# A mixer kernel with linear attention on one core: spans of 384 and 288 columns, other tilings of small matmuls, and sign words from ScalarE

## The chip, the core and the metric

The kernel runs on one core of a Trainium2 chip. The metric is the device time of one execution in microseconds; the median of three runs is compared. Five engines work beside each other, each with its own queue of instructions: TensorE (PE in the profile, with its weight loads as PEld), VectorE (DVE), ScalarE (ACT), GpSimd (POOL) and SyncE (SP), which issues the transfers.

## The reference

For 4 batches, 4 heads, 1088 positions and a head size of 32, the attention is linear: queries and keys go through a product of two small projections of 8 columns each (64 features), and the sums over positions are made once per head. The result is the input of an MLP-mixer, whose weights are shared by the batches.

```python
a, b = x @ S1.T, x @ S2.T                      # 8 columns each
phi(x) = outer(a, b).reshape(64)
kv = sum_s phi(k)[f] * v[d];  z = sum_s phi(k)[f]
x = (phi(q) @ kv) / (phi(q) @ z + 1e-6)        # heads side by side: 1088 x 128
h = relu(x.T @ w_tok1) @ w_tok2                # over positions, 256 hidden
u = x + h.T
out = u + relu(u @ w_ch1) @ w_ch2              # over channels, 1536 hidden
```

All inputs are float32.

## The kernel before, in words

**Weights.** The four weight matrices and the small matrix of S1 and S2 come as 64-bit doubles, two 32-bit words per number, and are turned into float32 on the chip, in 17 pieces of 256 to 512 columns (`convert`, L279 to L319) and in one of 64 columns. ScalarE writes the magnitude of the high word (`abs`, L293) and the scaled low word (`low`, L297); VectorE clamps the magnitude (`clamp`, L300), shifts it by three bits (`shift`, L304) and puts the sign bit in (`merge`, L307); GpSimd adds the low word (`add`, L311 and L313). Then ScalarE and one of VectorE and GpSimd split the result in a high and a low float32r half (`hi`, L394, and `lo`, L397). A product with full precision is then three matmuls of halves.

**Batches.** For each batch `keys` projects the keys (`K.p`), multiplies the projections on VectorE (`K.v`) and sums over positions on TensorE (`K.s`, L460): per pair of heads and tile of 128 positions two matmuls, each with the 64 features of one head as weights and 66 columns of values of both heads. Queries of batch 0 are projected on TensorE with the small matrix spread out so that 128 feature rows come out (`Q0.p`, L539), copied by ScalarE and multiplied by VectorE or GpSimd. Queries of the other batches are projected to 8 columns (`Q.p`, L505), written to memory and read back spread out by DMA (`Q.w`, `Q.r`), then multiplied (`Q.m`). `mixing` attends (`A.x`, L645), divides (`A.d`), and does the token mixing (`A.t`, `A.w`).

**Channel mixing.** The 4352 columns of all batches are cut into spans (`_spans`): three of batch 0 (384, 384, 320), then eight of 384 and one of 192. For each span and each of 12 hidden tiles there is a group of three matmuls into a hidden bank (`U.f`, L871), a ReLU on ScalarE (`U.h`, L875), its rest on VectorE (`U.l`, L878) and three matmuls into the output bank (`U.s`, L884).

**Order.** No scheduler chooses the order: `ORDER` is a list written out by hand, with an engine behind a colon where there is a choice. `Plan.run` emits it entry by entry, and each engine takes its own entries in that order. `Plan.run` also keeps a running estimate of times, and puts matmuls on the identity (`fill`, L272) into TensorE's queue where its estimate has a hole of over 400 ns.

## Time and profile before

| | us |
|---|---|
| median of three runs (lowest, highest) | 224.02 (223.56, 224.95) |
| the profiled execution's own time | 224.45 |
| its span, first to last instruction | 222.6 |
| TensorE busy, matmuls | 216.7 |
| VectorE busy | 151.1 |
| ScalarE busy | 115.0 |
| GpSimd busy | 60.7 |

An engine is busy while one of its instructions is under way. Matmuls overlap each other, so the mean duration of one (some 0.33 us for 384 columns) is not what it costs; the spacing of starts is. A row of the timeline or of the chain that covers several instructions ends in their count. "Idle before" is idle time of the engine and what ended it.

### The profile page before, as it was taken

The numbers are of one execution on the slowest core, as the hardware profiler recorded it, in microseconds if no ns is written. First come the engines' busy times: TensorE is split into PE (matmuls) and PEld (weight loads), VectorE is DVE, ScalarE is ACT, GpSimd is POOL, SyncE is SP. The second block draws the span as 40 slices with busy tenths as digits, with TensorE's granted clock in tenths as the row PEclk, the third lists the DMA queues.
The fourth block names the chain that finished last, engine by engine and source line by source line (L and its number), as shares of the span: only waits on it lengthen the run. The fifth ranks groups of instructions, "written<-read, shape, count | busy, mean of one in ns | idle before, by whom it ended". The sixth has DMA issues, their size and how long they took to land.

```text
span 222.6 us, 4807 instructions
## 1 busy us (share of the span) xinstructions
PE 216.7 (97%) x1854; PEld 205.5 (92%) x1854; DVE 151.1 (68%) x310; ACT 115.0 (52%) x269; POOL 60.7 (27%) x62
## 2 busy tenths in 40 slices
PE   7999999999999999999999999999999999999994
PEld 7767868789899999999999999999999999999994
DVE  2599999999779854786644667384556654665652
ACT  3488859865826343444533437253554455445441
POOL 2256585578961615102120505000000000000000
PEclk9999999999999999999999999999999999999999
DMA  6999899697059884249550100035000000020001
GB/s 193 417 406 406 248 361 349 214 259 213 9 116 170 256 167 79 65 111 172 197 168 0 38 0 3 0 141 141 3 0 3 35 3 0 0 71 3 35 0 53
DMA packets 10726, 28.41 MB, mean 128 GB/s; under 512 B 1360, under 2 KB 4688, under 8 KB 10704
## 3 DMA queue, kind: packets, MB, share of 16 engines
q1 hardware_dynamic: 10704, 28.11, 41.5%
q8 instruction: 14, 0.23, 0.4%
q14 instruction: 8, 0.07, 0.1%
HBM read 23.27 MB, written 4.83 MB: 126 GB/s over the span
## 4 chain that ended last, share of the span: by engine, by line
PE 79%; DMA 6%; DVE 6%; ACT 3%; issue 2%; SPq 1%; POOL 1%; POOLq 0%; ACTq 0%
PE ps_o L884 29%; PE ps_h L871 28%; DMA br<-rows 5%; PE ps_a L821 4%; PE ps_a L701 3%; PE ps_o L272 3%; PE ps_a L645 3%; PE ps_a L460 2%; DMA doubles<-wt 2%; DVE hl L878 2%; PE ps_a L539 1%; PE ps_h L539 1%; DVE k_p L443 1%; ACT tail L297 1%; PE ps_o L460 1%
## 5 line engine op out<-in xcount | busy, mean ns | idle before, releaser
L875 ACT ACTIVATE hh<-ps_h 128x384 fp32r<-128x384 f32 (+2 forms) x144 | 68.2, 475 | 84.4 <-PE ps_h L871 63.3
L878 DVE SCALAR_TENSOR_TENSOR hl<-ps_h,hh 128x384 fp32r<-128x384 f32 (+2 forms) x144 | 75.3, 532 | 50.3 <-ACT hh L875 46.0
L871 PE MATMUL ps_h<-uh,halves 128*128 128x384 f32 (+2 forms) x288 | 86.0, 333 | 0.6 <-DVE hl L878 0.5
L884 PE MATMUL ps_o<-hh,halves 128*128 128x384 f32 (+2 forms) x288 | 72.0, 332 | 0.0
L871 PEld LDWEIGHTS ps_h<-uh,halves 128*128 128x128 f32 x288 | 53.1, 188 | 1.8 <-DVE hl L878 1.0
L884 PEld LDWEIGHTS ps_o<-hh,halves 128*128 128x128 f32 x288 | 50.6, 188 | 0.6
L871 PE MATMUL ps_h<-ul,halves 128*128 128x384 f32 (+2 forms) x144 | 47.4, 329 | 0.0
L884 PE MATMUL ps_o<-hl,halves 128*128 128x384 f32 (+2 forms) x144 | 47.4, 329 | 0.0
L871 PEld LDWEIGHTS ps_h<-ul,halves 128*128 128x128 f32 x144 | 27.1, 188 | 0.0
L884 PEld LDWEIGHTS ps_o<-hl,halves 128*128 128x128 f32 x144 | 27.1, 188 | 0.0
L625 POOL TENSOR_TENSOR qp<-qp,br 128x544 f32<-128x544 f32 x9 | 13.2, 1484 | 15.9 <-DMA br<-rows 8.7
L311 POOL TENSOR_TENSOR whole<-c,tail 128x512 int32<-128x512 int32 (+3 forms) x11 | 11.7, 1063 | 9.6 <-DVE c L307 8.1
L669 POOL TENSOR_TENSOR xl<-x,xh 128x384 fp32r<-128x384 f32 x6 | 6.1, 1017 | 28.6 <-ACT xh L665 28.6
L293 ACT ACTIVATE c<-doubles 128x512 f32<-128x512 f32 (+3 forms) x17 | 10.3, 624 | 2.5 <-DMA doubles<-wt 2.5
L443 DVE TENSOR_TENSOR k_p<-ps_a,a_sb 128x1024 f32<-128x1024 f32 (+1 forms) x12 | 11.0, 947 | 0.0
L307 DVE SCALAR_TENSOR_TENSOR c<-doubles,ps_h 128x512 int32<-128x512 int32 (+3 forms) x17 | 10.4, 610 | 0.2
L297 ACT ACTIVATE tail<-doubles 128x512 int32<-128x512 uint32 (+3 forms) x17 | 10.4, 630 | 0.1
L304 DVE TENSOR_SCALAR ps_h<-c 128x512 int32<-128x512 int32 (+3 forms) x17 | 10.3, 615 | 0.1
L645 PEld LDWEIGHTS ps_a<-kvz,qp 128*64 128x64 f32 x288 | 9.0, 137 | 1.3 <-issue 0.5
L701 PE MATMUL ps_a<-halves,xh 128*128 128x256 f32 x54 | 10.0, 279 | 0.0
L300 DVE TENSOR_SCALAR c<-c 128x512 f32<-128x512 f32 (+3 forms) x17 | 8.6, 522 | 2.0 <-ACT c L293 1.9
L313 POOL TENSOR_TENSOR c<-c,tail 128x512 int32<-128x512 int32 x6 | 8.1, 1358 | 6.6 <-DVE c L307 3.2
(82 smaller groups left out, 242.2 us busy)
## 6 DMA issues: line engine op xcount, KB each, us to landing
qp<-rows SPq DMA_DIRECT2D x6, 544.0 KB, 8.6
br<-rows SPq DMA_DIRECT2D x12, 272.0 KB
doubles<-wc SPq DMA_DIRECT2D x6, 512.0 KB, 10.8
v_sb<-v SPq DMA_DIRECT2D x4, 594.0 KB, 4.6
k_sb<-kT SPq DMA_DIRECT2D x4, 576.0 KB
q_sb<-qT SPq DMA_DIRECT2D x4, 544.0 KB, 10.4
doubles<-wt SPq DMA_DIRECT2D x4, 512.0 KB, 7.0
xm<-xb SPq DMA_DIRECT2D x3, 576.0 KB, 9.2
```

Source lines behind the costliest of these rows:

```text
L293: nc.scalar.activation(f32(t["c"]), f32(high), AF.Abs)
L297: nc.scalar.activation(t["tail"], low.bitcast(U32), AF.Copy, scale=2.0 ** -29)
L307: nc.vector.scalar_tensor_tensor(t["c"], high, -(1 << 30), t["ps"], op0=ALU.bitwise_and, op1=ALU.bitwise_or)
L311: engines[e].tensor_tensor(dst(), t["c"], t["tail"], op=ALU.add)
L443: nc.vector.tensor_tensor(t["k_p"][:pn, t0 * H:t1 * H], a.unsqueeze(3).broadcast_to([pn, n, R, R]), t["sb", t0][:pn, :n].unsqueeze(2).broa ...
L625: engines[e].tensor_tensor(qp[:, p, cs], qp[:, p, cs], t["br"][:, p, cs], op=ALU.mult)
L645: nc.tensor.matmul(x_ps[c:c + 64, o:o + 2 * (D + 1)], lhsT=qp[:, p, s0 + c:s0 + c + 64], rhs=kvz_all[b % 2][:, p, :], start=True, stop=True,)
L701: nc.tensor.matmul(t["h_ps"][:, :DTOK], lhsT=t[l][:m, i, :], rhs=part(0, piece, r, j * DTOK, DTOK)[:m], start=(i == 0 and k == 0), stop=(i ...
L871: nc.tensor.matmul(h_ps[:, :cn], lhsT=part(2, at[2][e][0], l, at[2][e][1] * P, P), rhs=r[:, :cn], start=(m == 0), stop=(m == 2))
L875: nc.scalar.activation(t["hh"][:, :cn], t["h"][:, :cn], AF.Relu)
L878: nc.vector.scalar_tensor_tensor(t["hl"][:, :cn], t["h"][:, :cn], 0.0, f32(t["hh"][:, :cn]), op0=ALU.max, op1=ALU.subtract)
L884: nc.tensor.matmul(outs[i][:, :cn], lhsT=part(3, at[3][e][0], l, at[3][e][1] * P, P), rhs=r[:, :cn], start=(e == 0 and m == 0), stop=(e == ...
```

## The change

- The last two spans have 288 and 288 columns, not 384 and 192.
- The query projection of batch 0 uses 64 rows per head pair, so that its two halves lie on different row groups of TensorE. The sums of keys and values have 33 columns, one head's values, not 66; in batches 1 to 3 they are split once more, into 32 features each on four column groups. The projection of the queries of batches 1 to 3 is cut into 64 rows by 32 columns.
- `convert` scales the magnitude by a power of two, so that its clamp needs only an upper bound; the shift moves into `merge`, and the sign words are written apart (`sign`), either by ScalarE with a parametric ReLU, or by VectorE with a mask. 13 of 18 are given to ScalarE (small matrix included).
- Identity fills cover up to 512 columns with one matmul, and 36 small matmuls (`PAD`) stand behind the first four fills. They move the later matmuls in the stream of instructions.
- Loads are no longer chained in the plan, and `ORDER` is another one. Its part up to the eighth `U.f` group is shown for both kernels.

```diff
-    for n in (384,) * 8 + (192,):
+    for n in (384,) * 7 + (288, 288):
...
-s d00 q0 k0 d01 v0 d02 d03 d04 d10 d11 d20 d30 q1 d12 d13 s.abs s.low s.clamp s.shift s.merge s.add Q0.s0:dve Q0.s1:pool w00.abs w00.low w00.clamp
-w00.shift w00.merge w00.add Q0.p00 Q0.p20 Q0.a00 Q0.a20 w01.abs Q0.p01 Q0.a01 K0.p Q0.m00 Q0.m20 w01.clamp w01.shift w01.merge Q0.p11 Q0.b01 Q0.m01
-K0.c0 K0.c4 w01.low K0.c8 w01.add w02.abs s.rows w03.abs Q0.a11 Q0.b11 w04.abs K0.v0 K0.v4 K0.v8 w02.clamp w03.clamp w02.shift w04.clamp Q0.p10 K0.s00
-K0.s04 K0.s08 K0.s10 K0.s14 K0.s18 w10.abs Q0.a10 w02.low w02.merge w10.clamp w03.shift Q0.m10 w03.merge Q0.m11 Q0.p21 K0.kvz w03.low w02.add w04.low
-A0.x0 w03.add Q0.a21 Q0.b21 w10.low w11.abs w20.abs Q0.m21 A0.x1 w04.shift w10.shift A0.d0 A0.d1 w04.merge w11.clamp w04.add w10.merge w11.shift
-w20.clamp w11.merge Q1.p Q1.c0 w11.low w30.low w10.add w11.add w13.low w12.abs Q1.c1 w30.abs w20.low w12.low w13.abs A0.x2 A0.d2 A0.t0 A0.t1 A0.t2
-A0.relu A0.hT A0.hTh A0.u0 A0.w0 k1 d21 d31 Q1.w0 v1 Q1.w1 d14 d15 d22 d32 q2 w20.shift w12.clamp w30.clamp w20.merge w13.clamp w12.shift w30.shift
-w12.merge w13.shift w30.merge w20.add w20.hi A0.uh00 K1.p w12.add w20.lo:dve w30.add A0.ul00 w13.merge U0.f U0.f A0.u1 U0.f w13.add A0.w1 w00.hi K1.c0
-K1.c8 w30.hi U0.h U0.h w21.abs U0.h w21.low A0.uh11 w30.lo:pool K1.v0 K1.v8 U0.l U0.l w21.clamp U0.l w21.shift A0.ul11 w21.merge U0.s U0.s U0.s U1.f
-U1.f U1.f w04.hi K1.c4 w14.abs w22.abs w31.low U1.h w31.abs w21.add K1.v4 Q2.p K1.s U1.h w21.hi Q2.c0 U1.h w14.low Q2.c1 w15.low k2 K2.p U1.l
-w14.clamp w31.clamp w31.shift w22.clamp U1.l w31.merge U1.l w14.shift w14.merge w22.shift w22.merge Q1.r0None Q1.r00 Q1.r01 v2 Q1.r1None Q1.r10 Q1.r11
-Q2.w0 q3 k3 w21.lo:pool U0.f U0.f U1.s U1.s U1.s U0.f w31.add w32.abs w32.low K1.kvz w31.hi U0.h w14.add w15.abs U0.h U0.l w32.clamp U0.l w32.shift
...
+s q0 d00 d01 k0 s.low s.abs s.clamp s.sign:act s.merge s.add Q0.s0:dve Q0.s1:dve s.rows Q0.p00 Q0.p01 Q0.a00 Q0.m00 Q0.a01 Q0.b01 Q0.m01 w00.sign:dve
+Q0.p20 Q0.p21 w00.abs Q0.a20 Q0.m20 w00.clamp w01.abs Q0.a21 Q0.b21 v0 d04 d02 d03 w01.clamp w00.merge w01.sign:dve w01.merge Q0.p10 Q0.a10 K0.p
+Q0.p11 w01.low w00.low Q0.m21 w00.add w01.add K0.c0 K0.c4 w04.low w04.abs Q0.a11 K0.c8 Q0.b11 w02.abs w02.sign:act w03.abs w02.low K0.v0 K0.v4 K0.v8
+w02.clamp Q0.m10 d11 d20 d10 d12 q1 d13 d30 k1 Q0.m11 w02.merge w03.sign:act w03.clamp w04.clamp w03.merge K0.s00 K0.s04 K0.s08 K0.s10 K0.s14 K0.s18
+K0.kvz A0.x0 w04.sign:act w03.low w11.abs w11.sign:act w11.low w04.merge w02.add w04.add A0.d0 A0.x1 w11.clamp A0.d1 w11.merge A0.x2 A0.t0 A0.t1 A0.d2
+Q1.p w03.add w20.sign:act w11.add w10.abs w12.abs w20.low w20.abs w10.sign:act w10.low w13.abs w13.sign:act Q1.c0 Q1.c1 w13.low w12.low w10.clamp
+w20.clamp w12.clamp w10.merge w13.clamp w20.merge A0.t2 A0.relu A0.hT w12.sign:dve w12.merge w13.merge w10.add w20.add w30.sign:act w30.abs A0.hTh
+w30.clamp w30.merge w12.add K1.p d21 v1 d15 d31 d32 Q1.w0 Q1.w1 d14 d22 q2 Q1.r0None Q1.r00 Q1.r01 Q1.r1None Q1.r10 Q1.r11 w13.add w20.hi K1.c0
+w30.low w21.abs K1.c8 K1.c4 K1.v0 w21.clamp w20.lo:pool A0.u0 A0.w0 A0.u1 A0.w1 w21.sign:act A0.uh00 K1.v8 w21.merge A0.ul00 K1.v4 U0.f U0.f w04.hi
+w21.low w31.sign:act w31.abs A0.uh11 w30.add w21.add U0.h U0.h w30.hi K1.s A0.ul11 U0.l w31.clamp U0.l w31.merge w30.lo:pool w31.low w21.hi w31.add
+U0.f U1.f A0.u2 U0.h U1.h w15.abs w14.abs U0.l U1.l U1.f U0.s U1.f U0.s U0.s U1.s U1.h K1.kvz w31.hi w15.clamp w14.sign:dve w14.clamp U1.l
+w15.sign:act U1.h w21.lo:pool w14.merge w15.merge U1.l w32.abs w32.sign:act U0.f U0.f U1.s w32.clamp w32.merge w31.lo:pool U0.h U0.l w22.sign:dve Q2.p
...
+PAD = 36
...
-LEAST = 2.0 ** -15
-MOST = 122879.9921875
+REBIAS = 2.0 ** -112
+MOST = 2.0 ** -95 * (1 - 2.0 ** -24)
...
-            for _ in range(n):
-                nc.tensor.matmul(spare_ps[:, :P], lhsT=ident, rhs=ident, start=True, stop=True)
+            for w in [4] * (n // 4) + [1] * (n % 4):
+                nc.tensor.matmul(spare_ps[:, :w * P], lhsT=ident, rhs=ident.unsqueeze(1).broadcast_to([P, w, P]), start=True, stop=True)
...
-            nc.scalar.activation(f32(t["c"]), f32(high), AF.Abs)
+            nc.scalar.activation(f32(t["c"]), f32(high), AF.Abs, scale=REBIAS)
...
+        def sign(e):
+            t["ps"] = bank("ps_h")[:, :n].bitcast(I32)
+            if e == "act":
+                nc.scalar.activation(t["ps"], f32(high), AF.Prelu, scale=2.0 ** -19, alpha=2.0 ** 70)
+            else:
+                nc.vector.tensor_scalar(t["ps"], high, -(1 << 31), None, op0=ALU.bitwise_and)
+
         def clamp(_):
-            nc.vector.tensor_scalar(f32(t["c"]), f32(t["c"]), LEAST, MOST, op0=ALU.max, op1=ALU.min)
-
-        def shift(_):
-            t["ps"] = bank("ps_h").bitcast(I32)[:, :n]
-            nc.vector.tensor_scalar(t["ps"], t["c"], 3, 0x3FFFFFFF, op0=ALU.logical_shift_left, op1=ALU.bitwise_and)
+            nc.vector.tensor_scalar_min(f32(t["c"]), f32(t["c"]), MOST)
 
         def merge(_):
-            nc.vector.scalar_tensor_tensor(t["c"], high, -(1 << 30), t["ps"], op0=ALU.bitwise_and, op1=ALU.bitwise_or)
+            nc.vector.scalar_tensor_tensor(t["c"], t["c"], 3, t["ps"], op0=ALU.logical_shift_left, op1=ALU.bitwise_or)
...
+                    parts = 2 if b else 1
                     for j in range(2):
                         h = 2 * p + j
-                        nc.tensor.matmul(
-                            t["kv"][j * F:(j + 1) * F, p * 2 * (D + 1):(p + 1) * 2 * (D + 1)],
-                            lhsT=t["k_p"][:n, i * H + h].rearrange("p i j -> p (i j)"),
-                            rhs=t["v"][:n, i, 2 * p:2 * p + 2, :].rearrange("p h d -> p (h d)"),
-                            start=(i == 0), stop=(i == NT - 1),
-                        )
+                        for c in range(parts):
+                            o, m = j * F + c * F // parts, F // parts
+                            nc.tensor.matmul(
+                                t["kv"][o:o + m, p * (D + 1):(p + 1) * (D + 1)],
+                                lhsT=t["k_p"][:n, i * H + h, c * R // parts:(c + 1) * R // parts].rearrange("p i j -> p (i j)"),
+                                rhs=t["v"][:n, i, h, :], start=(i == 0), stop=(i == NT - 1),
+                            )
...
-    def project_queries(q, r, ps):
-        for j in range(2):
-            c = 2 * j + r
-            nc.tensor.matmul(ps[j * 64:(j + 1) * 64, :QC], lhsT=box["s_rows"], rhs=q[:, c * QC:(c + 1) * QC], start=True, stop=True)
+    def project_queries(q, ps):
+        for c in range(4):
+            for p in range(2):
+                rows = slice(p * 64, (p + 1) * 64)
+                nc.tensor.matmul(ps[p][c * 32:(c + 1) * 32, :QC], lhsT=box["s_rows"][rows], rhs=q[rows, c * QC:(c + 1) * QC], start=True, stop=True)
...
+                    for p in range(2):
+                        rows = slice(p * 64, (p + 1) * 64)
+                        nc.tensor.matmul(
+                            t[kind, g, p][:, :cn], lhsT=t["s"][rows, kind, 2 * p:2 * p + 2].rearrange("p h i j -> p (h i j)"),
+                            rhs=box["q_sb", 0][rows, cs], start=True, stop=True,
+                        )
...
+    for i in range(PAD):
+        c = i % 4 * 32
+        nc.tensor.matmul(spare_ps[c:c + 32, :8], lhsT=ident[:, c:c + 32], rhs=ident[:, :8], start=True, stop=True)
```

## Rows read from the trace of the kernel before

**Rows 1.** The page: busy time per engine, the queue of TensorE's instructions

```profile
PE 216.7 (97%) x1854; PEld 205.5 (92%) x1854; DVE 151.1 (68%) x310; ACT 115.0 (52%) x269; POOL 60.7 (27%) x62
...
q8 instruction: 14, 0.23, 0.4%
```

**Rows 2.** Busy time (count) by stretch: PE, PEld, DVE, ACT, POOL; clock; DMA

```profile
5.54:44.04 38.50, 37.28 (x452) 29.55 (x450) 35.50 (x71) 30.26 (x72) 20.83 (x18) 1.00 0.93 342
44.04:219.60 175.56, 175.21 (x1386) 171.79 (x1386) 114.15 (x235) 83.05 (x195) 38.24 (x34) 1.00 0.31 80
```

**Rows 3.** The chain of waits around 47 us: start, length, what

```profile
44.62 0.69 DVE c L307
...
47.07 0.79 PE ps_h L871 x3
```

**Rows 4.** TensorE's timeline, first 30 us: start, length, instruction, count

```profile
1.36 6.70 PE L272 MATMUL ps_o<-ident 128*128 128x128 f32 x32 [1.36 <-POOL ident masks.py:199]
7.90 0.81 PE L539 MATMUL ps_a<-q_sb,s_spread 128*128 128x384 f32 x2
...
15.63 2.32 PE L460 MATMUL ps_o<-v_sb,k_p 128*64 128x66 f32 x72
...
20.71 0.94 PE L272 MATMUL ps_o<-ident 128*128 128x128 f32 x6
...
27.68 0.38 PE L272 MATMUL ps_o<-ident 128*128 128x128 f32 x2
```

**Rows 5.** TensorE's timeline, a wait, and the second matmul of the eighth group

```profile
43.11 0.45 PE L871 MATMUL ps_h<-uh,halves 128*128 128x384 f32 x1 [0.35 <-DVE hl L878]
...
44.31 0.34 PE L871 MATMUL ps_h<-ul,halves 128*128 128x384 f32 x1
```

**Rows 6.** The chain of waits, matmuls of 320, 384 and 192 columns

```profile
80.38 0.88 PE ps_h L871 x6
...
191.21 1.56 PE ps_h L871 x9
...
214.18 0.67 PE ps_h L871 x6
```

**Rows 7.** Busy time of L539, the query projection of batch 0

```profile
7.00:24.00 17.00, 8.01 (x24) 4.32 (x24) 1.00 1.03 408
```

**Rows 8.** TensorE's timeline: a look ending at 56.68; sums of batch 2 and their surroundings

```profile
56.67 0.28 PE L460 MATMUL ps_a<-v_sb,k_p 128*64 128x66 f32 x2
...
81.19 1.14 PE L505 MATMUL ps_a<-q_sb,s_rows 128*64 128x272 f32 x8
82.15 2.27 PE L460 MATMUL ps_a<-v_sb,k_p 128*64 128x66 f32 x72
84.35 0.56 PE L884 MATMUL ps_o<-hh,halves 128*128 128x320 f32 x2
84.75 0.31 PE L884 MATMUL ps_o<-hl,halves 128*128 128x320 f32 x1
```

**Rows 9.** Groups by form: low word and table load (ScalarE), shift (VectorE); busy us, mean ns

```profile
L297 ACT ACTIVATE tail<-doubles 128x512 int32<-128x512 uint32 x10 | 6.9, 686 | 0.0
...
L297 ACT ACTIVATE tail<-doubles 128x384 int32<-128x384 uint32 x4 | 2.3, 572 | 0.1
...
L293 ACT ACT_TABLE_LOAD x1 | 1.3, 1283 | 0.7 <-PEq L983 0.7
...
L304 DVE TENSOR_SCALAR ps_h<-c 128x512 int32<-128x512 int32 x10 | 6.9, 686 | 0.1
...
L304 DVE TENSOR_SCALAR ps_h<-c 128x384 int32<-128x384 int32 x4 | 2.2, 552 | 0.0
```

**Rows 10.** ScalarE's timeline: two conversions that follow each other

```profile
5.54 0.67 ACT L293 ACTIVATE c<-doubles 128x512 f32<-128x512 f32 x1 [2.54 <-DMA doubles<-wt]
6.11 0.67 ACT L297 ACTIVATE tail<-doubles 128x512 int32<-128x512 uint32 x1
```

**Rows 11.** The end: the last add, which waits for the last matmul

```profile
219.57 0.35 DVE L909 TENSOR_TENSOR o_sb<-us,ps_o 128x192 f32<-128x192 f32 x1 [0.62 <-PE ps_o L884]
```

More of the change, by code (lines that the diff above doesn't have):

```diff
@@ L166, in run @@
         free = dict.fromkeys(LATE, 0.0)
[L167 removed]
+        free["sp"], free["act"], free["pe"] = 1060.0, 2000.0, 1400.0 + 427 * WARM + 35 * PAD
         dma, mode, port = 2800.0, 0, 0.0
@@ L276, in emit @@
             nc.sync.dma_start(dst(), src)
-        op = plan.add(name, {"sp": 475.0}, emit, (), takes, uses, boost, order=after)
+        op = plan.add(name, {"sp": 475.0}, emit, (), takes, uses, boost)
         op.bytes, op.rate = nbytes, 395.0
@@ L316, in convert @@
         r = plan.add(name + ".low", act_sb(n), rest, [loaded], [tail_hold])
+        g = plan.add(name + ".sign", act(n) | dve(n), sign, [loaded], [ps_hold])
         m = plan.add(name + ".clamp", dve2(n), clamp, [a], (), [c_hold], port=True)
-        m = plan.add(name + ".shift", dve(n), shift, [m], [ps_hold], [c_hold])
-        m = plan.add(name + ".merge", dve(n), merge, [m], (), [c_hold, ps_hold])
+        m = plan.add(name + ".merge", dve(n), merge, [m, g], (), [c_hold, ps_hold])
         ways = {"dve": 69 + 2.084 * n} if keep else {"pool": 141 + 2.15 * n}
@@ L490, in all_sums @@
                     sums(p, 0, NT)(_)
-            last = plan.add(f"{n}.s", {"pe": 2 * NT * 117.0}, all_sums, products + [v_loaded[b]], [kv_hold], [kp_hold, v_hold[b]], boost, 1)
+            last = plan.add(f"{n}.s", {"pe": 1150.0}, all_sums, products + [v_loaded[b]], [kv_hold], [kp_hold, v_hold[b]], boost, 5)
         for p in () if b else range(2):
@@ L530, in queries_on_pe, with project, emit @@
         for g, (c0, cn) in enumerate(CHUNKS):
-            for p in range(2):
-                br_hold = Hold("ar")
-                a_hold, b_hold, ar_hold = Hold("ps_a"), Hold("ps_h"), Hold("ar")
-                cs = slice(c0, c0 + cn)
-                def project(_, g=g, p=p, cs=cs, cn=cn):
-                    for kind, name in enumerate(("ps_a", "ps_h")):
-                        x = t[kind, g, p] = bank(name)
-                        nc.tensor.matmul(x[:, :cn], lhsT=t["s"][:, kind, 2 * p:2 * p + 2].rearrange("p h i j -> p (h i j)"), rhs=box["q_sb", 0][:, cs], start=True, stop=True)
+            cs = slice(c0, c0 + cn)
+            a_holds, b_holds = [Hold("ps_a") for _ in range(2)], [Hold("ps_h") for _ in range(2)]
+            def project(kind):
+                def emit(_, g=g, cs=cs, cn=cn):
+                    for p in range(2):
+                        t[kind, g, p] = bank("ps_h" if kind else "ps_a")
+                    for p in range(2):
+                        rows = slice(p * 64, (p + 1) * 64)
+                        nc.tensor.matmul(
+                            t[kind, g, p][:, :cn], lhsT=t["s"][rows, kind, 2 * p:2 * p + 2].rearrange("p h i j -> p (h i j)"),
+                            rhs=box["q_sb", 0][rows, cs], start=True, stop=True,
+                        )
+                return emit
+            projected = []
+            for kind, holds in ((0, a_holds), (1, b_holds)):
+                projected.append(plan.add(f"Q0.p{g}{kind}", {"pe": cn * 1.675 + 8}, project(kind), [q_loaded[0]] + spreads, holds, [q_hold[0]], 0.0, 3, order=projected[:1]))
+            for p in range(2):
+                br_hold, ar_hold = Hold("ar"), Hold("ar")
+                a_hold, b_hold = a_holds[p], b_holds[p]
                 def slot():
@@ L583, in project @@
                 t["ps", r] = bank("ps_a")
-                project_queries(box["q_sb", b], r, t["ps", r])
-        p = plan.add(f"{n}.p", {"pe": 2 * 2 * QC / 1.2}, project, [q_loaded[b], s_rows_done], ps, [q_hold[b]], boost, 1, order=[after])
+            project_queries(box["q_sb", b], [t["ps", r] for r in range(2)])
+        p = plan.add(f"{n}.p", {"pe": 2 * (QC / 1.2 + 40)}, project, [q_loaded[b], s_rows_done], ps, [q_hold[b]], boost, 2, order=[after])
         for r in range(2):
```

91 lines of the change are left out of this document (45 added, 46 removed).

## The prediction

> **What bounds the kernel now.** Begin with the page. TensorE is busy for 216.7 of 222.6 us, VectorE for 151.1, ScalarE for 115.0 [rows 1]. A busy TensorE may still be held back, so the table by stretches comes next. From 5.54 to 44.04 us VectorE is busy for 35.50 of 38.50 us and ScalarE for 30.26; after 44.04 VectorE needs 114 of 175.6 us while TensorE has no hole [rows 2]. So there are two stages: a start in which the weights are converted and three engines are nearly full, and a rest in which TensorE alone counts. The chain of waits agrees: up to 47 us it runs through VectorE's conversions, then through matmuls only [rows 3].
>
> How much of the start does TensorE lose? Its timeline has 32 matmuls on the identity, which compute nothing, from 1.36 to 7.90, and eight more later, 0.94 and 0.38 us; the first true work is the query projection at 7.90 [rows 4]. That is 8 us at the head and 1.3 in the middle; the waits for other engines that I find later are short, the longest 0.35 us [rows 5]. Spacings times counts give the same: about 210 us of work for a last matmul that ends near 219.5 [rows 11]. The kernel is bound by TensorE's work, and the start is so well packed that VectorE's list ends just in time for it.
>
> **The change, part by part.** All durations are from this profiled execution, 224.45 us with a span of 222.6 inside; the median of the runs is 224.02, 0.4 lower, and I put my result between them.
>
> *Spans.* 384 + 192 columns become 288 + 288. A matmul of 384 columns takes 1.56/9 = 0.173 us, one of 320 0.147, one of 192 0.112 [rows 6]; 64 columns less save 0.026, but the next 128 save only 0.035 where 0.053 would be in proportion: at 192 a floor holds. 288 lies on the slope: 0.147 - 32 x 0.0004 = 0.133. Each span has 72: 72 x (0.173 + 0.112) = 20.5 becomes 144 x 0.133 = 19.2, -1.3 us, all of it at the end where TensorE is alone. Bounds: 0.130, in proportion to 384 columns (a gain of 1.8), and 0.1425, halfway between the rows of 192 and 384 (no gain).
>
> *Query projection of batch 0.* 24 matmuls, 8.0 us busy, about 7.8 by spacing [rows 7]. They now use 64 rows each, the two halves on different row groups. If the halves run side by side, 3.9 is left; if not, 7.8. No row here has two row groups at work; I take the first, since two column groups do run side by side [rows 8], and keep the second.
>
> *Sums of keys and values.* Per batch 1 to 3, 72 matmuls of 66 columns take 2.2 us (82.15 to 84.35), 31 ns each [rows 8]; now 144 of 33 columns on four column groups of 32 instead of two of 64. If streaming sets the pace, half the columns on twice the groups need a quarter of 31 ns each: 1.1 us. If issue does, 31 ns each: 4.5. What decides is whether 31 ns is streaming or issue. A look that ends 20 ns into the burst shows two matmuls already begun [rows 8], so issue can be faster than 20 ns each; I take 1.3, near the streamed end, -0.9 per batch, -2.7 in all. Batch 0 keeps two groups at 33 columns: 2.3 [rows 4] becomes 1.2, -1.1.
>
> The Trainium skill speaks against this: "TensorE: Matmul & The Clock Gate" (Wait - 56ns, not 53.3ns?) says that starts of matmuls never come closer than about 25 ns, however few the columns. By it the sums would take an estimated 144 x 25 ns = 3.6 us, 1.4 more than now, and the total below would become 222.3, two batches of it counting in full. The two starts within 20 ns say otherwise for matmuls on different column groups; no row shows a long run of them.
>
> *Projection of batches 1 to 3.* 8 matmuls of 272 columns last 0.96 us from the first start to the sums' first [rows 8]; 16 on eight tiles of 64 x 32: 0.6 if row groups overlap, 0.96 if not. -1.0 in all.
>
> *Modes.* A change of tiling costs TensorE a little: after the sums two 320-wide matmuls take from 84.35 to 84.75 instead of 0.29 [rows 8], 0.1 more and about as much in front. Counted from the written order there are 22 such changes now and 27 after: +1.0.
>
> TensorE's work so falls by 1.3 + 3.9 + 1.1 + 2.7 + 1.0 - 1.0 = 9.0, to 201.
>
> *Sign words.* VectorE loses the shift of 12 weight pieces and the small matrix, seven of them at 0.686 us, three at 0.552, and on the line through both one of 320 columns at 0.485 and one of 256 at 0.42 [rows 9], 7.4 us; it gains from GpSimd one spread of 256 columns, 0.4 by the same line. In five pieces the shift becomes a mask of the same kind at the same price. The clamp loses one of its two constants but still reads and writes every column: zero, and as a bound a whole shift per piece, 0.686. ScalarE gains the twelve: with the present word copies as their like, 7 x 0.686 + 3 x 0.572 + 0.51 + 0.46 = 7.5 by duration [rows 9], and since its instructions start 0.57 apart though they last 0.67 [rows 10], 6.3 us. The new merge waits for the sign beside the clamp, so behind ScalarE's queue; behind the merge stand the add on GpSimd, then the halves, then a matmul. The order puts each sign next to its magnitude, which the clamp needs anyway.
>
> *Loads.* The same bytes; the queries of batch 0 are issued first, where the first weight piece now is. That piece reaches ScalarE at 5.54 [rows 10]; the queries, issued next, are used at 7.90 [rows 4]. Swapped, projection starts near 5.7: -2.2 at the head; ScalarE's first conversion is that much later, but it copies projections meanwhile. Key loads of batch 1 go ahead of four weight pieces, and the queries' round trip to memory ahead of the next keys. SyncE's queue waits there for ScalarE's copies with three loads behind; as now, and nothing before the second span needs them. The 36 small matmuls and the wider fills stand where TensorE waits for the queries anyway: zero, and if that cover goes, some 1.3 us. TensorE's instructions come in 14 fetches [rows 1]; that is 3708 matmuls and weight loads / 14 = 265 a fetch, and a burst of the new sums is 288 in 1.3 us. None stalls now, and where the blocks' edges fall I can't see: zero, and as a bound three stalls of 1 us, the page giving a fetch 0.4% of 16 x 222.6 us / 14 = 1.0.
>
> **Sum.** If nothing but TensorE counted: -9.0, -2.2 at the head, -1.3 of middle fills, and +0.4 for a wider last add and store (0.35 us and then some 2.7 us to the end of the span now [rows 11]): -12, 212.4.
>
> But ScalarE takes VectorE's place. Take the eighth group of hidden-layer matmuls, at 44.04 now [rows 5]. Counted from the order with the durations by form, VectorE's list ahead of it shrinks from 40.8 to 32.9 us; ScalarE's, less 0.1 us of overlap each, grows from 28.0 (68 instructions) to 34.0 (79), of which 1 lies before 5.54. So 5.54 + 33 = 38.5 is the earliest if ScalarE never waits (it is idle for 8.2 of 38.5 us now [rows 2]); TensorE's own list would have allowed 33. Gain there: 5.5 us. Behind the eighth group TensorE's list falls from 175.6 to 174.0, since key and query projections move behind it. -5.5 - 1.6 + 0.4 = -6.7: 217.7.
>
> **The rivals.**
> - *TensorE alone decides*: ScalarE's list can be deferred further, as it ran ahead of need by some 2.7 us of entries at 44.04. 212.4; for it, the row of idle ScalarE; against, the count above. 20%.
> - *ScalarE holds the start*: its whole busy time to 44.04 plus the signs is 36.5 of 38.5 us [rows 2], so with 2 us of waits left nothing is gained there. Left: the end's 1.3, two batches of sums 1.8, projections 0.7, less modes: -3.2, 221.2. 15%.
> - *ScalarE over-full*, the other side. If all 8.2 us of its present idle time stay (waits on matmuls, GpSimd and loads) and the 6.3 us of signs come on top, the eighth group slips to 50.3, and 224.45 + 6.3 - 3.2 = 227.5. It turns the sign of the change once more than 5.1 us of the 8.2 remain. For it: signs go into the engine that feeds both others, and the new merge waits for them; against: VectorE, for which it waited in turn, has 7.8 us less to do. 6%.
> - *Row groups don't overlap*: projections stay at 7.8; TensorE's 5.7 us of slack in the start hide most: 219. 5%.
> - *The sums are issued, not streamed*: at today's 31 ns, 4.5 us instead of the assumed 1.3; batch 1 lies in the slack, the other two cost 6.4: 224.1. The present spacing speaks for it, the two starts within 20 ns against. 3%, and 3% for something between, 222.3.
> - *A table switch for every sign*, slower too. The one table load now costs 1.283 us [rows 9]; if the ReLU with a slope had another table than magnitude and copy, 13 signs would bring up to 26 loads, 33 us on ScalarE in the start: 245. All present functions run with one load. 4%. "ScalarE: Activation LUTs" in the Trainium skill (Table sets: the hidden batching unit) says that cheap functions are in every set, without naming this one.
>
> **How the numbers follow.** 44% for the forecast (216 to 219.5). The predicted time is its 217.7. Range 212 to 222.5: from TensorE alone to ScalarE holding, with the bounds of spans, row groups and fetches in between; it leaves out the slower cases, the slow sums and a tail below 212, 0.2 together. About 1%, 2.2 us, is what can be told from no change here (under 221.8 faster, over 226.3 slower). Faster: 44 + 20 + 5 + 12 of the 15 = 0.81. Within 1%: 3 + 3 + 3 = 0.09. Slower: 6 + 4 = 0.10.
>
> **What would show it.** First projection matmul near 5.7 and half as long in sum; sums near 1.3 us per batch in a burst of 144; a 288-wide matmul at 0.133; one table load; ScalarE over 90% busy from 6 to 40 us and VectorE near 75%; the eighth group near 39. Matmuls of the sums spaced by 25 ns or more, identity matmuls or idle TensorE between 10 and 40 us for more than 6 us, or a second table load would make it wrong.

## The result and the profile after

The changed kernel takes 221.56 us (median of 4 runs, 220.57 to 222.56) against 224.15 of the kernel before beside it: ratio 0.9881, interval 0.9833 to 0.9929. That is 2.6 us faster; I forecast 217.7, which is 6.7 below the profiled execution and 6.3 below the median. The direction and the range held, the size did not. The profiled execution took 221.22 us with a span of 219.2, against 224.45 and 222.6.

The page of after, busy times and the queue of TensorE's instructions:

```profile
PE 210.4 (96%) x2152; PEld 196.4 (90%) x2152; DVE 145.2 (66%) x290; ACT 120.0 (55%) x283; POOL 66.3 (30%) x69
...
q8 instruction: 17, 0.28, 0.5%
```

TensorE and VectorE lost some 6 us each, ScalarE and GpSimd gained 5 to 6 [rows 1]: the work moved as intended, and yet of TensorE's 6.3 us only 2.6 reach the end (3.4 between the two profiled spans). The table by stretches, with the columns of [rows 2], tells where the rest stays:

```profile
5.54:44.04 38.50, 34.32 (x495) 26.11 (x495) 32.77 (x62) 33.85 (x79) 23.22 (x20) 1.00 0.96 338
44.04:219.60 175.56, 171.85 (x1581) 167.67 (x1580) 111.33 (x224) 83.87 (x200) 41.89 (x40) 1.00 0.29 81
```

In the start TensorE's busy time fell by 3 us and the stretch got hardly shorter. I follow the first matmuls of four of the 144 hidden-layer groups (us from the start of the span), and give the ratio to before; "off" is what a ratio says in us of 224.0. Some executions are a few per cent longer at a lower granted clock; the ratios leave those out, the medians don't, so I compare by ratios. An interval reaches about 1 us to either side, so a difference of 1 us between two ratios counts only where the groups' times agree with it.

```
                 1st    8th   12th  144th   ratio   interval          off
before          31.97  44.04  49.73  217.70
after           33.49  43.27  48.35  213.73  0.9881  0.9833 0.9929   -2.7
e1 no sign      35.13  44.42  50.24  217.02  1.0009  0.9979 1.0039   +0.2
e2 head         33.33  43.09  48.15  214.41  0.9898  0.9850 0.9946   -2.3
e3 no small mm  32.30  47.27  52.26  218.91  1.0007  0.9961 1.0052   +0.2
e4 spans        33.74  43.52  48.61  216.71  0.9937  0.9905 0.9970   -1.4
e5 sign cut     32.26  41.59  46.58  212.04  0.9814  0.9778 0.9850   -4.2
e6 clamp cut    32.19  41.55  46.69  212.23  0.9786  0.9741 0.9831   -4.8
e7 both cut     31.02  39.89  44.89  211.06  0.9728  0.9699 0.9757   -6.1
e8 mid          31.61  42.97  48.97  214.45  0.9872  0.9822 0.9922   -2.9
e9 late         32.99  41.60  49.94  215.39  1.0017  0.9983 1.0050   +0.4
e10 late, mid   32.00  40.63  48.95  216.02  0.9932  0.9901 0.9964   -1.5
e11 all rows    33.54  43.30  48.35  214.02  0.9898  0.9870 0.9926   -2.3
e12 sums        32.45  42.21  47.27  214.09  0.9924  0.9880 0.9968   -1.7
e13 orders      34.70  44.36  49.35  215.45  0.9897  0.9868 0.9926   -2.3
e14 orders, mid 33.90  43.56  48.54  213.92  0.9874  0.9833 0.9915   -2.8
e15 VectorE     37.06  48.08  53.07  219.33  1.0103  1.0059 1.0146   +2.3
e16 one swap    33.19  42.08  47.08  212.36  0.9831  0.9790 0.9871   -3.8
e17 swap, mid   31.96  40.81  45.80  211.07  0.9807  0.9774 0.9841   -4.3
```

Between the two profiled executions the change gained 0.8 us up to the eighth group (forecast 5.5) and 3.2 from there to the 144th (forecast 1.6); behind that it lost 0.5, since the last span is wider (forecast 0.4). TensorE's timeline of after:

```profile
6.02 1.65 PE L552 MATMUL ps_a<-q_sb,s_spread 64*128 64x384 f32 x4
...
13.00 0.92 PE L552 MATMUL ps_h<-q_sb,s_spread 64*128 64x384 f32 x4
...
16.24 1.83 PE L467 MATMUL ps_o<-v_sb,k_p 128*64 128x33 f32 x56 [0.45 <-DVE k_p L447]
...
35.11 1.70 PE L467 MATMUL ps_a<-v_sb,k_p 128*32 128x33 f32 x144
...
42.64 0.44 PE L893 MATMUL ps_h<-uh,halves 128*128 128x384 f32 x1 [1.14 <-DVE c L311]
...
79.62 1.43 PE L467 MATMUL ps_a<-v_sb,k_p 128*32 128x33 f32 x144
80.98 0.69 PE L512 MATMUL ps_a<-q_sb,s_rows 64*32 64x272 f32 x16
```

Queries start at 6.02 instead of 7.90 [rows 4]; a burst of sums takes 1.4 to 1.7 us instead of 2.27 [rows 8]; the seventh group, at 42.64, waits for a merge on VectorE. The chain of waits in front of it:

```profile
39.48 0.92 issue
40.40 0.48 DVE ps_h L305
40.88 0.23 DVE c L308
41.10 0.48 DVE hl L900
41.58 0.02 issue
41.60 0.47 ACT ps_h L303
42.08 0.02 issue
42.10 0.50 DVE c L311
42.60 0.04 issue
42.64 1.03 PE ps_h L893 x4
```

The "issue" is not idle time of VectorE. All engines' timeline shows its clamp of w15 beside GpSimd's `w21.lo`:

```profile
38.99 1.30 POOL L401 TENSOR_TENSOR halves<-c,halves 128x512 fp32r<-128x512 f32 x1
...
39.08 1.39 DVE L308 TENSOR_SCALAR c<-c 128x320 f32<-128x320 f32 x1
...
40.79 0.31 DVE L308 TENSOR_SCALAR c<-c 128x320 f32<-128x320 f32 x1
40.81 1.44 POOL L401 TENSOR_TENSOR halves<-c,halves 128x512 fp32r<-128x512 f32 x1 [0.52 <-ACT halves L398]
```

A clamp of the same size takes 0.31 us a little later, begun between two instructions of GpSimd. So the first one stands waiting for some 1.1 us, until GpSimd is done. I call what they wait for "the port", as the kernel's plan does; the traces show the waiting, not the port. Behind it come `w14.sign`, `w14.clamp` and `U1.l`; only `U1.l` frees the PSUM bank that `w15.sign` on ScalarE writes; only then can w15 be merged, which frees the bank of the seventh group. There are three such banks (`ps_h`), for hidden groups and sign words alike.

### The profile page after: what moved, and what is told of

Same layout as the page of the kernel before. It is cut to its first block, busy times and chain, and to the rows that moved or that the text cites. A ratio compares the mean times of both kernels' runs of the same rounds, so it can differ in the third digit from the quotient of the medians.

```text
span 219.2 us, 5399 instructions
## 1 busy us (share of the span) xinstructions
PE 210.4 (96%) x2152; PEld 196.4 (90%) x2152; DVE 145.2 (66%) x290; ACT 120.0 (55%) x283; POOL 66.3 (30%) x69
## 4 chain that ended last, share of the span: by engine, by line
PE 82%; ACT 5%; DMA 5%; DVE 4%; SPq 1%; issue 1%; POOL 0%; DVEq 0%
PE ps_h L893 33%; PE ps_o L906 32%; PE ps_a L723 5%; DMA doubles<-wt 5%; PE ps_a L843 4%; PE ps_a L667 3%; PE ps_a L467 2%; ACT c L294 2%; ACT tail L298 1%; PE ps_a L428 1%; SPq L277 1%; ACT ps_h L303 1%; PE ps_a L839 1%; DVE c L308 1%; DVE c L311 1%
## 5 line engine op out<-in xcount | busy, mean ns | idle before, releaser
L906 PE MATMUL ps_o<-hh,halves 128*128 128x384 f32 (+2 forms) x288 | 71.1, 330 | 0.0
L817 POOL TENSOR_TENSOR ul<-us,uh 128x64 fp32r<-128x64 f32 (+5 forms) x9 | 5.7, 640 | 38.4 <-ACT uh L814 38.4
L647 POOL TENSOR_TENSOR qp<-qp,br 128x544 f32<-128x544 f32 x8 | 11.3, 1424 | 16.7 <-DMA br<-rows 8.8
L691 POOL TENSOR_TENSOR xl<-x,xh 128x384 fp32r<-128x384 f32 x6 | 6.8, 1138 | 31.3 <-ACT xh L687 19.0
L315 POOL TENSOR_TENSOR whole<-c,tail 128x512 int32<-128x512 int32 (+3 forms) x11 | 11.7, 1078 | 11.1 <-DVE c L308 4.4
L401 POOL TENSOR_TENSOR halves<-whole,halves 128x384 fp32r<-128x384 f32 (+3 forms) x9 | 9.9, 1118 | 4.4 <-DVE xb L777 4.4
L311 DVE SCALAR_TENSOR_TENSOR c<-c,ps_h 128x512 int32<-128x512 int32 (+3 forms) x17 | 10.2, 610 | 0.4
L308 DVE TENSOR_SCALAR c<-c 128x512 f32<-128x512 f32 (+3 forms) x17 | 10.0, 610 | 0.5 <-ACT c L294 0.5
```

The costliest lines, as they stand in the source:

```text
L308: nc.vector.tensor_scalar_min(f32(t["c"]), f32(t["c"]), MOST)
L311: nc.vector.scalar_tensor_tensor(t["c"], t["c"], 3, t["ps"], op0=ALU.logical_shift_left, op1=ALU.bitwise_or)
L315: engines[e].tensor_tensor(dst(), t["c"], t["tail"], op=ALU.add)
L906: nc.tensor.matmul(outs[i][:, :cn], lhsT=part(3, at[3][e][0], l, at[3][e][1] * P, P), rhs=r[:, :cn], start=(e == 0 and m == 0), stop=(e == ...
```

## The experiments

An engine's list is what it has to do, in the order written. Theory A: ScalarE's list, now with signs, sets the start. Theory B: VectorE's order and the port that it shares with GpSimd set it. Rivals on the way: the head, TensorE's work, its instruction blocks.

**e1, no sign words from ScalarE.**
```diff
-t["ps"] = bank("ps_h")[:, :n].bitcast(I32); nc.scalar.activation(..., AF.Prelu, ...)
+t["ps"] = unsigned.broadcast_to([P, n])   # a zero word in SBUF
```


> The changed kernel without the twelve sign writes of the weights on ScalarE: the merge reads a constant zero word instead, so the signs of those weights are left out; all else, order and loads included, is kept (the planner's estimate is told of zero cost there). Theory A (ScalarE's list with the signs sets the start): the first group of hidden-layer matmuls, at 33.5 us in the changed kernel, comes 4 to 5 us earlier, the eighth group goes from 43.3 to 38 to 40, and the time falls by 3.5 to 5.5 us, to about 217. Theory B (VectorE's order and its waits for the port it shares with GpSimd set the start): the first group moves by under 1.5 us and the time by under 1.5. Theory C (weights land too late): no change at all.

The kernel leaves out the signs of twelve pieces. It got slower than after, by 2.9 us, though ScalarE was relieved; but the experiment changed a second thing. The merge no longer reads PSUM, and now it too waits beside GpSimd. Its timeline:

```profile
26.62 1.00 POOL L320 TENSOR_TENSOR whole<-c,tail 128x384 int32<-128x384 int32 x1 [1.43 <-ACT abT L618]
26.67 1.50 DVE L316 SCALAR_TENSOR_TENSOR c<-c,unsigned 128x512 int32<-128x512 int32 x1
```

The same merge with the sign in PSUM takes 0.68 in after, with GpSimd at work beside it as without; with both operands in SBUF it takes 0.68 alone, and four times 1.37 to 1.50 beside GpSimd. So e1 says much about the port and nothing clean about A; e5 repeats it with PSUM kept.

**e2, the head's order undone.** `d00` is loaded before `q0`, `w00.abs` and `w00.low` stand ahead of `Q0.a00`.
```diff
-s q0 d00 d01 k0 ... Q0.p00 Q0.p01 Q0.a00 ... Q0.p21 w00.abs ... w01.low w00.low
+s d00 q0 d01 k0 ... w00.abs w00.low Q0.p00 Q0.p01 Q0.a00 ... Q0.p21 ... w01.low
```


> The changed kernel with the head of the kernel before: the first weight piece is loaded ahead of the queries, and its two ScalarE conversions stand ahead of the first copy of a projection, so that ScalarE begins its run at about 5.5 us instead of 7.7. Theory A (ScalarE's list sets the start, and it starts late): ScalarE has 1.1 us of work done in time now idle, so the first group comes 1 us earlier and the time falls by 0.5 to 1.2 us; projections start up to 2 us later and are hidden. Theory D (the early projection is worth its place): the projections' copies come 2 us later, the chain over keys and attention with them, and the time rises by 1 to 2 us.

Within the intervals the same as after, and the eighth group at 43.09: whether queries or weights come first is worth nothing here. ScalarE does its first two conversions while it would otherwise wait for the projections, and the queries start 1.3 us later, at 7.36; neither reaches the eighth group.

**e3, no small matmuls at the head.**
```diff
-PAD = 36
+PAD = 0
```


> The changed kernel without the 36 small matmuls; the planner's estimate puts full-width identity matmuls in their place where it sees a hole. Theory E (the small matmuls leave TensorE's clock low longer): the granted clock rises before 7.8 us, the first two projection groups take 0.32 us per pair instead of 0.64, ScalarE's first copy comes 0.6 to 1 us earlier and the time falls by 0.3 to 1 us. Theory F (their place in the stream of instructions matters): fetches of instruction blocks fall elsewhere, bursts of sums or attention stall, and the time rises by 0.5 to 3 us.

The first group comes 1.2 us earlier, the whole is 2.8 us slower than after. TensorE's timeline, the table by stretches and the instruction queue from 37.2 to 40.8 us show why, in an execution of 226.47 us (the twelve lie between 222.49 and 228.42):

```profile
36.90 0.49 PE L748 MATMUL ps_a<-ident,x 128*128 128x128 f32 x3
40.85 0.69 PE L893 MATMUL ps_h<-uh,halves 128*128 128x384 f32 x1 [3.46 <-DVE c L308]
```
```profile
38.00:42.00 4.00, 1.15 (x4) 1.15 (x5) 1.86 (x4) 0.36 (x1) 1.04 (x1) 0.73 0.81 216
42.00:46.00 4.00, 4.00 (x14) 4.00 (x13) 2.12 (x5) 2.99 (x8) 1.28 (x1) 0.50 0.54 198
```
```profile
q8 instruction: 1, 0.02, 2.3%
```

TensorE stands for 3.5 us, and the engine named as releaser is not it: that clamp ended at 39.86, and ScalarE, VectorE and GpSimd run out of work too. What runs is one transfer of the instruction queue, from 38.17 to 39.49, a few matmuls behind the burst of 288 instructions (matmuls and weight loads) of the sums of batch 1. I read it so: without the 36 small matmuls the burst meets the edge of a block and uses up the next one before another is there; e8 tests it. The granted clock, 1.00 until then, falls to 0.50 (1.2 GHz) during the standstill and costs more: the stall is not the clock's doing. That it stands in every execution of e3, one trace can't show.

**e4, spans of 384 and 192.**
```diff
-    for n in (384,) * 7 + (288, 288):
+    for n in (384,) * 8 + (192,):
```


> The changed kernel with the spans of the kernel before, 384 and 192 at the end. All theories: the last two spans are on TensorE alone, 72 x (0.173 + 0.112) against 144 x 0.133 us, so the time rises by 1.2 to 1.4 us, less up to 0.4 for a shorter last add and store.

1.3 us slower than after, as forecast for this part (1.3), though the intervals overlap. The chain of after settles it: nine matmuls of 288 columns take 1.20 us, 0.133 each, the forecast's figure.

```profile
206.29 1.20 PE ps_h L893 x9
```

**e5, one column of every sign; e6, 32 columns of every clamp; e7, both.**
```diff
-nc.scalar.activation(t["ps"], f32(high), AF.Prelu, ...)
+nc.scalar.activation(t["ps"][:, :1], f32(high)[:, :1], AF.Prelu, ...); t["ps"] = t["ps"][:, :1].broadcast_to([P, n])
```
```diff
-nc.vector.tensor_scalar_min(f32(t["c"]), f32(t["c"]), MOST)
+nc.vector.tensor_scalar_min(f32(t["c"])[:, :32], f32(t["c"])[:, :32], MOST)
```


> ScalarE writes only the first column of every sign word, and the merge reads that one column, still in PSUM, for the whole piece; the signs of the result are therefore those of the first column. ScalarE loses some 0.5 us in each of ten pieces ahead of the eighth hidden-layer group (5 us), VectorE and GpSimd keep their instructions. Theory A, ScalarE's list with the signs sets the start: the eighth group comes at 38.5 to 40 us instead of 43.3, the whole takes 217 to 218.5. Theory B, VectorE's order and the port that it shares with GpSimd set it: the eighth group at 42.3 to 43.3, the whole 220.5 to 221.6.

> The clamp touches 32 columns of a piece instead of all (the others are left unclamped). It takes 0.26 to 0.43 us alone and up to 1.4 us when it stands waiting; twelve of them. Theory B (VectorE and the shared port): some 4 us of VectorE and its stalls go, the eighth group at 39.5 to 41 us, the whole 217.5 to 219.5. Theory A (ScalarE's list): the eighth group stays at 42.5 to 43.3, the whole at 220.5 to 221.6.

> Both cuts at once: one column of sign, 32 columns of clamp. If either engine alone held the start, the result is that of the cut which helped, and no more. If the two hold it in turns, neither cut alone gives much and this one gives the whole 4 to 5 us: the eighth group near 38.5, the whole 217. If neither holds it (loads, matmuls or GpSimd do), it stays at 43 and 221.

e5 leaves out all signs but those of the first column of a piece, e6 most of each clamp. Neither A nor B alone: relieving ScalarE brings the eighth group 1.7 us forward, relieving VectorE 1.7, both 3.4, and the whole comes down by 1.5, 2.1 and 3.4 us by the ratios. Each to its own eighth group, the stretches of after, e5, e6 and e7:

```profile
5.54:43.27 37.73, 33.55 (x492) 25.34 (x491) 32.10 (x61) 33.08 (x77) 23.22 (x20) 1.00 0.96 341
```
```profile
5.54:41.59 36.05, 33.11 (x492) 25.45 (x491) 31.70 (x61) 28.97 (x77) 23.33 (x20) 1.00 1.01 353
```
```profile
5.54:41.55 36.01, 34.11 (x491) 25.85 (x491) 28.55 (x61) 32.70 (x77) 22.67 (x20) 1.00 1.00 355
```
```profile
5.54:39.89 34.35, 33.06 (x491) 25.57 (x491) 27.55 (x61) 28.88 (x77) 22.59 (x20) 1.00 1.00 360
```

ScalarE lost 4.1 us in e5 and 1.7 of it arrived; in e7 both engines are shorter by over 4 and still idle for 5.5 and 6.8 us. They work in turns on the same pieces, so each waits for the other, and neither works through its list without a gap.

**e8, the small matmuls in the middle**, ahead of `A0.t1`, where TensorE waits anyway.
```diff
-    for i in range(PAD): ... matmul(spare_ps...)      # ahead of plan.run
+            if name == "A0.t1": pad()                 # in plan.run
```


> The 36 small matmuls that shift TensorE's instruction blocks stand ahead of the first mixing projection A0.t1, where TensorE waits for VectorE by about 1 us anyway, instead of at the head. Behind that place every matmul keeps its place in the blocks. If the stall of 3.5 us behind the sums of batch 1 in the kernel without them (e3) came from the blocks' edges, it is absent here; and if the head's 1.2 us that e3 gained at the first hidden-layer group came from their absence at the head, it is kept: first group near 32.3, eighth near 42.2, the whole 220.2 to 220.8. If the clock or the head's order made e3 slow, the stall of 3.5 us behind the sums of batch 1 shows again and the whole is 223.5 to 224.5.

The stall of e3 is gone with the blocks back in place. The first group comes 1.9 us earlier, the eighth only 0.3: two clamps waiting beside GpSimd, 1.46 and 1.41 us, hold the seventh group until 41.85. Its runs lie between 220.4 and 223.9 us; in the profiled one the granted clock fell from 1.00 to 0.5 for 3.4 us behind that wait.

**e9, w14 and w15 converted later; e10, the same on e8.**
```diff
-w15.abs w14.abs ... w15.clamp w14.sign:dve w14.clamp ... w15.sign:act ... w14.merge w15.merge ... U0.f U0.f
+U0.f U0.f ... w22.merge U0.h U0.l w15.abs w14.abs w14.sign:dve w15.sign:act w15.clamp w14.clamp w14.merge w15.merge
```


> Conversion of the two last pieces of the second token weights (w14, w15: magnitude, sign, clamp, merge, add) is moved behind the hidden-layer groups that follow it; the rest stays. In the kernel after, the seventh group waits 1.48 us (41.16 to 42.64), until w15 is merged: the sign word of w15 lies in one of the three PSUM banks that hidden groups take, from its sign to its merge. If that bank is what holds the seventh and eighth group, they come 1.2 to 1.5 us earlier (eighth near 42) and the whole takes 219.8 to 220.3. If the list of VectorE in front of it holds (1.9 us of w14 and w15 work less is not what counts), the wait moves to the conversion of w31 or w21, the eighth group stays within 0.4 us and the whole at 220.8 to 221.6.

> e9 and e8 together: w14 and w15 late, and the 36 small matmuls in the middle instead of at the head. The head's 1.9 us (first group at 31.6) was given back in e8 in a wait of 2.6 us before the seventh group. If the bank of w15's sign word was that wait, it is gone, the eighth group comes near 40.2 and the whole takes 218 to 218.8. If the conversions behind it hold, it stays at 42 and 220 to 221.

The eighth group comes 1.7 us earlier, as the bank says, and the wait comes back ahead of the eleventh, larger. TensorE's timeline of e9:

```profile
46.79 0.33 PE L893 MATMUL ps_h<-uh,halves 128*128 128x384 f32 x1
49.31 0.44 PE L893 MATMUL ps_h<-uh,halves 128*128 128x384 f32 x1 [2.20 <-DVE c L311]
```

There the two clamps put off stand beside GpSimd, 2.15 us for both. Work put off is still in front of the next groups that want the same banks. My expectation stopped at the eighth group and missed that, for e10 as well: there the eighth group comes at 40.63, near the 40.2 expected, the eleventh waits just as long, and the whole is 1.1 us slower than after, not some 3 faster.

**e11, the queries of batch 0 with all 128 rows.**
```diff
-                        rows = slice(p * 64, (p + 1) * 64)
+                        rows = slice(0, P)
```


> The query projection of batch 0 multiplies all 128 rows in every matmul, as before the change (half of the rows of the spread matrix are zero, so the result is the same): no two matmuls on different row groups side by side, 24 matmuls of 0.32 us after each other, some 3.7 us of TensorE more. If TensorE's work counted in the start, the whole is 224.5 to 225.3. If conversions set it, the projections lie beside them and only the first two, for which ScalarE waits at the head, count: the eighth group 0.3 to 1.3 us later, the whole 221.4 to 222.6.

Eighth group 43.30 instead of 43.27, the whole 0.4 us slower: what row groups save lies wholly beside the conversions. In the profiled executions that is 2.0 us (7.75 us busy here, 5.77 in after).

**e12, the sums on two column groups.**
```diff
-                    parts = 2 if b else 1
+                    parts = 1
```


> The sums of keys and values of batches 1 to 3 with one part of 66 columns on two column groups, 72 matmuls instead of 144 of 33 on four: 2.2 us per batch instead of 1.45. The sums of batch 1 lie in the start that conversions hold (nothing or little there), those of batches 2 and 3 count in full: +1.5, the whole 222.3 to 223.1. It also takes 144 matmuls and weight loads per batch out of TensorE's instruction blocks: if a block's edge then falls into a burst, up to 1.4 us more for each fetch that is waited for; if the bursts of 288 instructions were themselves waiting for blocks, as little as 220.8.

By ratio 1.0 us slower than after, with intervals that overlap; in the profiled execution 1.4 between the eighth and the 144th group: 0.7 for each of the two batches behind it. At the first group that execution is already 1.0 us ahead of after, and I call that luck: its head came earlier (last section).

**e15, all sign words as masks on VectorE.**
```diff
-... w02.sign:act ... w03.sign:act ... w32.sign:act
+... w02.sign:dve ... w03.sign:dve ... w32.sign:dve
```


> All sign words are masks on VectorE, none on ScalarE (the part of the change that loads ScalarE is undone). Eleven more on VectorE and eleven fewer on ScalarE ahead of the eighth group, 0.5 to 0.7 us each, some 6.5 us. If VectorE's list with its waits at the shared port holds the start as much as e5 to e7 say, the eighth group comes 4 to 6 us later than 43.3 and the whole takes 225 to 227.5, slower than before the change. If ScalarE's list alone had held, the eighth group would come at 40 to 42 and the whole at 218.5 to 220.5.

Slower than before the change, by 1.0%, and 5.0 us slower than after. The sign words on ScalarE are what makes this change a gain: without them, in an order written for them, the other parts are lost in a start that ends at 48.

**e13, four swaps in the queues; e14, the same on e8.**
```diff
-w30.sign:act w30.abs A0.hTh | w13.add w20.hi ... w21.clamp w20.lo:pool ... w21.sign:act A0.uh00 K1.v8 w21.merge A0.ul00
+A0.hTh w30.sign:act w30.abs | w20.hi ... w20.lo:pool w13.add ... A0.uh00 w21.sign:act A0.ul00 w21.clamp K1.v8 w21.merge
-w15.clamp w14.sign:dve w14.clamp U1.l w15.sign:act
+w14.sign:dve U1.l w15.clamp w14.clamp w15.sign:act
```


> Only places in the queues change, no work: A0.hTh ahead of the sign and magnitude of w30 on ScalarE; w20.lo ahead of w13.add on GpSimd; A0.uh00 and A0.ul00 ahead of the sign and clamp of w21; the second U1.l ahead of the clamp of w15, which in the kernel after waits 1.1 us for the port while w21.lo runs on GpSimd, so that the bank for w15's sign is free 1.1 us earlier. If the start is held by waits of the two conversion engines for each other and for the port, 0.5 to 0.8 us come back at the first group and 1.1 more at the seventh: eighth group at 41.6 to 42.2, the whole 219.8 to 220.4. If it is held by the sheer sum of the lists, the eighth group and those to the twelfth move by under 0.4 and the whole stays at 221.2 to 221.9.

> e13 with the 36 small matmuls in the middle as in e8. TensorE's clock rises earlier and the first group came 1.9 us earlier in e8, but a wait of 2.6 us ahead of the seventh group took it back. If the orders of e13 shorten that wait: eighth group 40 to 41, the whole 218.5 to 219.5, a version faster than both kernels. If not: the whole 220.5 to 222.

Both missed what I expected if waits hold the start (eighth group at 41.6 to 42.2 and at 40 to 41). In e13 the wait ahead of the seventh group halves, 1.48 to 0.73 us, but the first group comes 1.2 us later: the clamp of w21 now falls beside GpSimd's `w30.add` and takes 1.39 us instead of 0.62, among others. e14 shows the same, 0.8 us earlier up to the twelfth group. Which of the first three swaps cost what, I did not take apart.

**e16, the last swap alone; e17, the same on e8.**
```diff
-w15.clamp w14.sign:dve w14.clamp U1.l w15.sign:act
+w14.sign:dve U1.l w15.clamp w14.clamp w15.sign:act
```


> Of the orders of e13 only the last: on VectorE the mask of w14 and the second U1.l stand ahead of the clamp of w15. In e13 the wait ahead of the seventh group fell from 1.48 to 0.73 us while the other moves cost 1.2 us at the first group. Alone it should leave the first group where it is (33.5) and bring the eighth to 42.4 to 42.9 and the whole to 220.6 to 221.2; if it is the sum of the lists alone that holds, the gain is gone again by the twelfth group (48.2 to 48.4 us) and the whole stays at 221.2 to 221.9.

> e16 with the 36 small matmuls in the middle. First group near 31.6 as in e8; the wait of 2.6 us ahead of the seventh group, in e8 a clamp of 1.32 us and what stood behind it, falls to about 1.7: eighth group near 42, the whole 219.8 to 220.8 where TensorE's clock does not fall in that wait. If e8's eighth group at 43 was set by the conversions' sum, 220.5 to 222.

One swap on VectorE gives 1.1 us by the ratios, whose intervals overlap; the groups from the eighth to the 144th come 1.2 to 1.4 us earlier. With it the small matmuls can go to the middle as well: e17 takes 219.70 us (218.62 to 219.94), ratio 0.9807, against after 0.9881, 1.7 us less; the two intervals overlap a little, and the profiled execution is the fastest of four. The timeline of e17 at the place of the chain above:

```profile
37.54 0.49 DVE L312 TENSOR_SCALAR ps_h<-doubles 128x320 int32<-128x320 int32 x1
...
38.15 0.56 DVE L907 SCALAR_TENSOR_TENSOR hl<-ps_h,hh 128x384 fp32r<-128x384 f32 x1
...
38.62 0.58 DVE L315 TENSOR_SCALAR c<-c 128x320 f32<-128x320 f32 x2
...
38.98 0.46 ACT L310 ACTIVATE ps_h<-doubles 128x320 int32<-128x320 f32 x1
```

`U1.l` (L907) is done before the clamps (L315), which now fall between two GpSimd instructions, 0.58 us for two; the sign on ScalarE follows at once.

## Why the forecast was off

**The step that failed** is "5.54 + 33 = 38.5 is the earliest if ScalarE never waits", taken as the time of the eighth group, which came at 43.27. ScalarE's list was right: 33.08 us busy from 5.54 to 43.27. The condition was wrong: it waits for 4.65 us, the first 2.2 in one piece, since with the queries first it has nothing to do until 7.71 ("it copies projections meanwhile" came too late for that), the rest for VectorE, GpSimd and banks. The first 2.2 alone are not the cause: e2 fills part of them and gains 0.2. I had asked which engine's list is longer and let the longer one run without a gap; VectorE's (32.9 forecast, 32.10 measured) was just as long. Two engines at 85 and 88% that pass every piece back and forth are together the bound, and e5, e6 and e7 show it: each alone gives 1.7, both 3.4. Only with both lists shorter by the 4 us of e7 is the forecast's 217.7 nearly met (218.04). That the waits can be cut with the lists left alone shows in e17: ScalarE is busy for 32.89 us and VectorE for 31.47 up to an eighth group at 40.81, though its early head has a part in that.

**What I costed at nothing.** "The clamp loses one of its two constants but still reads and writes every column: zero" was right alone (0.42 or 0.43 us for 512 columns before and after), but three clamps ahead of the eighth group, of w04, w11 and w15, stand at the port for about 1 us each (1.37 to 1.41 us). The kernel before had two such waits there, in VectorE's timeline:

```profile
23.77 1.06 DVE L300 TENSOR_SCALAR c<-c 128x512 f32<-128x512 f32 x1
...
40.22 1.31 DVE L300 TENSOR_SCALAR c<-c 128x512 f32<-128x512 f32 x1
```

So the waiting is not new; added up over all clamps ahead of the eighth group it grew from some 1.8 to 3.9 us. "The new merge waits for the sign beside the clamp, so behind ScalarE's queue" I had seen, not that the sign holds a hidden group's bank from its writing to the merge. The shift did so too, but VectorE wrote and merged it; now the hold spans two engines. That is the 1.5 us ahead of the seventh group (e9, e16).

**The parts.** Spans: forecast -1.3, e4 1.3. Sums: 1.3 us per burst forecast, 1.4 to 1.7 busy; e12 gives 0.7 per batch where I forecast 0.9. Projections 0.6, measured 0.69 with the last one's length in it. Queries on row groups: the halves start together and a pair takes the time of one, but the projection is busy for 5.77 us, not 3.9, since its first pairs come 0.5 to 0.8 us apart instead of 0.32; either way the gain is hidden (e11). They start at 6.02, forecast 5.7, and the 2.2 us at the head are worth nothing (e2). Sums of batch 0, forecast 1.2, stayed as they were: 56 matmuls of 33 columns start in 1.83 us, the same 30 ns apart as with 66 [rows 4]. Half the columns on the same two column groups save nothing; twice the groups do. One table load, as forecast. Behind the eighth group TensorE's list fell by 3.2 us instead of 1.6, by the spacing of starts: sums of two batches -1.7, hidden and output groups -2.6, projections moved there +1.5, the rest -0.3. So what came on top of the forecast lies in the groups, and I did not take it apart; without it the total would have missed by more. The sums of batch 1 stand ahead of the eighth group in both kernels; the burst at 56.67 [rows 8] is that of batch 2.

**A reading to put right.** Behind 47 us the chain of waits before does not run "through matmuls only": from 62.44 to 76.64 it goes over the queries' way through memory (a transfer of 10.16 us) and GpSimd. TensorE had other work meanwhile, 175.21 of 175.56 us busy [rows 2], so the two stages stand.

**The rule on starts.** The Trainium skill, "TensorE: Matmul & The Clock Gate" (Wait - 56ns, not 53.3ns?), would have spaced starts by 25 ns or more, an estimated 3.6 us for a burst. The trace has 144 in 1.43 us, 10 ns each, on four column groups; the measurement decides, as the prediction had it.

**The rivals.** The nearest in time was "ScalarE holds the start" (221.2), with the wrong owner: e5 takes its signs away and frees only 1.7 us, and e15 shows that giving them back to VectorE costs 5. The instruction blocks were costed at zero with "three stalls of 1 us" as a bound: in after none shows, in e3 one of 3.5 us does. So by the ratios the placed blocks are worth some 2.8 us against the same kernel without them.

## What to carry to other kernels

When two engines convert the same pieces in turns, the stage ends neither with the longer list nor when one list gets shorter: take both lists, add the waits at shared resources, and don't expect all of what one engine saves (here 1.7 of some 4 us). Before moving an operation to an idler engine, look at what its output occupies until it is used, here a PSUM bank that a matmul group needs. When a wait is cut by putting work off, follow it to the next user of the same resource.
